# The last third of a written-out order: other neighbours for TensorE, other engines for some words, other PSUM slots

## The chip, the cores and the metric

The kernel runs on one core of one Trainium2 chip. The metric is device time in microseconds, the median of several runs. TensorE (PE) multiplies matrices out of SBUF into PSUM, VectorE (DVE) and ScalarE (ACT) do elementwise work, GpSimd (POOL) issues the DMAs that add while they move, and SyncE (SP) issues all other DMAs. Each engine takes its own instructions in order and meets the others through semaphores. PE's array is used in tiles: whole (128x128), or in parts of 128x64, 128x32, 64x128 or 64x64 rows by columns. Every matmul carries its tile; two neighbours with different tiles are a change of tile.

## The reference

A gated linear recurrence with complex decay feeds a maxout network of three branches.

```python
mag = np.sqrt(a_re * a_re + a_im * a_im)
scale = np.minimum(mag, 0.999) / (mag + 1e-06)
a_re_n, a_im_n = (a_re * scale, a_im * scale)
for t in range(S):
    ar, ai = (a_re_n[:, :, t, :, None], a_im_n[:, :, t, :, None])
    new_re = ar * S_re - ai * S_im
    new_im = ar * S_im + ai * S_re
    kv = np.einsum('bhd,bhe->bhde', k[:, :, t], v[:, :, t])
    S_re, S_im = (new_re + kv, new_im)
    y[:, :, t] = np.einsum('bhd,bhde->bhe', q[:, :, t], S_re)
...
x = np.ascontiguousarray(attn_out.transpose(0, 2, 1, 3)).reshape(B * S, H * D)
h = np.maximum(np.maximum(x @ w1, x @ w2), x @ w3)
return (h @ w_out).astype(np.float32)
```

The sizes are 4 batches, 8 heads, 768 steps, head width 48; x is 3072 by 384, the hidden width 768; all is float32.

## The kernel before

The 768 steps of a sequence are cut into six pieces of 128, and two batches go together, so that there are twelve groups (0 to 11), each with two halves x and y of 128 tokens. A group goes through these stages:

- loads: `Lr`, `Li` (a_re and a_im, one DMA of 192 KB for each half), `Lk`, `Lq`, `Lv` (four DMAs of 48 KB for each half), all on SP;
- gates on whole groups (`sqr`, `sqi`, `add`, `lnL`, `expw`, `expe`, `lne`, `relu`, `Lnop`, `abs`, `addw`, `lnw`, `expL`, `mulai`, `mulw`, `stt`, `xor`, `half`, `atan`, `turn`): logarithms of the magnitudes and the angles. `Lnop` and `addw` are adds; as a rule a DMA on POOL does them;
- sums over time as matmuls: `sums`, `F` (logarithms) and `cs` (angles), then exponentials (`En`, `Ek`, `Eq`, `f0` to `f3`) on ACT and sines (`t`, `nf`, `af`, `sa`, `sb`). `Cd` carries an angle into the next piece by a small DMA on POOL;
- `mk`, `mq`, `uk`, `uq`: k and q times decay and turned by the angle, on DVE; `tpk`, `tpq`: transposes on PE; `Kc`, `Qc`: copies of these from PSUM;
- `A`, `B`: scores on PE, which `g0` to `g3` (DVE, predicated copies) and `b0`, `b1` (ACT) put together in `atm`; `dk` and `h0` to `h3`: the state; `y`: outputs on PE; `x`: their copy into the features;
- the network: `U01` to `U12` on PE (two halves of the hidden width by three branches), `u01` to `u12` the maxima, then the output product in Strassen's form: `S1` to `S4` on DVE, products `P1` to `P7`, `Px`, `Py` on PE, sums `r1`, `r6`, `r75`, `r57`, `ox`, `oy` on DVE (r1 on ACT), and `Dx`, `Dy`, the output DMAs on SP.

Nothing of this order is left to a scheduler. `SCHEDULE` is a text of 1880 words, each a stage and its group, such as `U01:7`; `run` (called for each word in turn) issues that stage's instructions, and the class `Bound` ties every instruction of an engine to the one before it. So the words give the order on each of the five engines, and how the engines interleave follows from semaphores. Two more lists go with it. `SLOTS` has one digit for each of 304 PSUM tiles in the order in which they are asked for: which of four slots of two banks (0, 2, 4, 6) the tile takes; the first matmul of a tile waits until the last reader of the tile before it in that slot is done. `OTHER` names the words that do not run on their usual engine: copies, absolute values, maxima and `relu` then go to DVE instead of ACT, `Lnop` and `addw` to DVE instead of a DMA of POOL.

```python
ps = psum.tile([P, 2, 512], FP, tag="ps" + next(slots), name=nm)
...
(pool if other() else dve).memset(t[L64 // 2:L64], 0.0)
...
if other():
    dve.tensor_copy(out=out, in_=in_)
else:
    act.copy(out=out, in_=in_)
```

Each k or q half has one SBUF buffer (`kqs`), which the next group's load may fill after `uk` or `uq` has read it; v has four buffers, a_re and a_im two each. Nearly all instructions carry line 201, that of the helper that issues them, so the profile is read by tile names: `up` is a U product, `op` the P products, `xhx` features and hidden values, `ot` the output rows, `tp` transposes.

Around the words that the prediction follows, before:

```
... tpky:8 P5:6 ... QGy:7 g0y:7 g1y:7 ... tpkx:8 ... Lqx:9 ... Lix:10 ... Lvx:8 ... Lkx:9 ... U11:7 ... mkx:9 ... U01:7 ... turn:9 ... tpqy:8 ... u02:7 ... Fx:9 ... Lqy:9 Lky:9
... Ax:10 ... U02:9 ... U12:9 Bx:10 atan:11 Cdy:10 Cdx:10 turn:11 Ay:10 ... yx:10 QBy:10 g0y:10 g1y:10 g2y:10 xx:10 S3:9 csy:11 csx:11 ... g3y:10
```

Of the kernel before, what the change touches and what calls it, by code (L numbers as in the profile page):

```python
# [91 lines left out]
Ekx:9 Lix:10 Lvx:8 sqi:10 Lkx:9 mkx:9 Eqx:9 QBx:8 u11:7 mqx:9 Q2x:8 U01:7 Cdx:8 atan:9 u01:7 add:10 lnL:10 Eqy:9 expe:10
U02:7 turn:9 tpqy:8 Qcy:8 dkx:8 relu:10 u02:7 h1x:8 Fx:9 Dy:6 h2x:8 Dx:6 f1x:9 f0x:9 Ax:8 h3x:8 Bx:8 g0x:8 g1x:8 U12:7
g2x:8 g3x:8 lne:10 Q2y:8 f3x:9 b0x:8 f2x:9 h0x:9 Lqy:9 Q1y:8 csy:9 ty:9 u12:7 S3:7 csx:9 nfy:9 expw:10 tx:9 b1x:8 S1:7
P1:7 r1:7 QBy:8 S2:7 nfx:9 KBy:8 sbx:9 afy:9 Ay:8 g0y:8 g1y:8 afx:9 g2y:8 g3y:8 Lky:9 yx:8 xx:8 sax:9 say:9 ukx:9 abs:10
By:8 h0y:8 sby:9 mky:9 P6:7 uqx:9 P7:7 mqy:9 P5:7 r6:7 S4:7 Py:7 b0y:8 Px:7 r75:7 r57:7 QGy:8 P4:7 oy:7 tpqx:9 tpkx:9
Lnop:10 Kcx:9 b1y:8 sumsx:10 kEnx:9 Qcx:9 Q1x:9 dky:8 h1y:8 h2y:8 h3y:8 Enx:10 uky:9 addw:10 lnw:10 Lkx:10 P2:7 expL:10
P3:7 Ekx:10 ox:7 KBx:9 yy:8 xy:8 Fy:9 f0y:9 f1y:9 QGx:9 f2y:9 Lvx:9 f3y:9 dkx:9 Eqx:10 QBx:9 U01:8 mkx:10 u01:8 Q2x:9
Ax:9 xor:10 half:10 h1x:9 Lvy:9 Bx:9 uqy:9 h2x:9 h3x:9 U11:8 g0x:9 Liy:11 g1x:9 Dy:7 g2x:9 g3x:9 Lqx:10 mqx:10 Cdy:9
u11:8 Fx:10 b0x:9 b1x:9 tpky:9 tpqy:9 kEny:9 Lry:11 mulw:10 mulai:10 stt:10 Dx:7 f1x:10 f3x:10 Qcy:9 Kcy:9 Q2y:9 U02:8  # L100
u02:8 f2x:10 U12:8 Lrx:11 sqr:11 Cdx:9 S3:8 atan:10 turn:10 f0x:10 Lix:11 yx:9 sqi:11 add:11 lnL:11 xx:9 expe:11 csy:10
xor:11 ty:10 csx:10 u12:8 S1:8 KBy:9 sumsy:10 nfy:10 Eny:10 Eky:10 S2:8 Q1y:9 QBy:9 afy:10 Eqy:10 Lqy:10 dky:9 P5:8
tx:10 lne:11 P6:8 P7:8 Ay:9 h0y:9 nfx:10 h1y:9 By:9 QGy:9 h2y:9 h3y:9 g0y:9 sbx:10 g1y:9 g2y:9 relu:11 afx:10 sax:10
ukx:10 g3y:9 P1:8 S4:8 r1:8 say:10 sby:10 mqy:10 r6:8 r75:8 b0y:9 b1y:9 expw:11 Py:8 P4:8 r57:8 Px:8 uqx:10 yy:9 xy:9
Fy:10 abs:11 f2y:10 Lky:10 oy:8 tpkx:10 kEnx:10 tpqx:10 f0y:10 f1y:10 f3y:10 uqy:10 Qcx:10 Lnop:11 P2:8 Dy:8 mky:10
Kcx:10 Q1x:10 addw:11 QGx:10 Lvx:10 P3:8 ox:8 U11:9 QBx:10 u11:9 sumsx:11 Enx:11 sumsy:11 half:11 uky:10 tpqy:10 Ekx:11
Q2x:10 Eqx:11 Lkx:11 tpky:10 Qcy:10 Kcy:10 Q2y:10 mkx:11 kEny:10 KBx:10 Lqx:11 U01:9 mqx:11 u01:9 Eny:11 h0x:10 dkx:10
h1x:10 Lvy:10 Eqy:11 Eky:11 lnw:11 expL:11 Fx:11 Ax:10 h2x:10 h3x:10 f3x:11 Q1y:10 f0x:11 U02:9 g0x:10 f2x:11 g1x:10
g2x:10 Dx:8 mulw:11 g3x:10 mulai:11 stt:11 f1x:11 U12:9 Bx:10 atan:11 Cdy:10 Cdx:10 turn:11 Ay:10 b0x:10 u02:9 u12:9
b1x:10 yx:10 QBy:10 g0y:10 g1y:10 g2y:10 xx:10 S3:9 csy:11 csx:11 S1:9 Lqy:11 P1:9 Lky:11 g3y:10 ty:11 mky:11 nfy:11  # L110
afy:11 say:11 S2:9 tx:11 nfx:11 P7:9 sby:11 P5:9 P6:9 uky:11 KBy:10 By:10 h0y:10 b0y:10 dky:10 Fy:11 mqy:11 b1y:10 S4:9
r1:9 sbx:11 h1y:10 h2y:10 h3y:10 afx:11 sax:11 r6:9 Px:9 Py:9 P2:9 P3:9 QGy:10 f0y:11 r75:9 uqy:11 r57:9 f2y:11 f3y:11
Lvx:11 uqx:11 Lvy:11 P4:9 yy:10 oy:9 ox:9 tpqx:11 f1y:11 xy:10 Qcx:11 ukx:11 tpkx:11 tpky:11 Kcy:11 tpqy:11 Qcy:11
U01:10 Q2y:11 u01:10 Q1x:11 QGx:11 Kcx:11 U11:10 Dx:9 QBx:11 h0y:11 Q2x:11 kEnx:11 KBx:11 U02:10 u11:10 kEny:11 dky:11
dkx:11 u02:10 S3:10 Ax:11 Dy:9 g0x:11 Q1y:11 h0x:11 h1x:11 h1y:11 U12:10 u12:10 Ay:11 S1:10 g0y:11 g1y:11 g1x:11 Bx:11
P1:10 g2x:11 P7:10 P5:10 g3x:11 b1x:11 b0x:11 yx:11 xx:11 QBy:11 g2y:11 g3y:11 KBy:11 By:11 S2:10 S4:10 P6:10 r1:10
# [6 lines left out]
0240624024202406402024604642064262624062046420640426240260620406404624624620620260264064262464046042
0624060202264204602604204624604602204600406204240620420460246260246202460246024062624640406204602602
6402466024240642460246026042064264064240246060206426040260046024240604204060420602640424062420242002
4202
# [916 lines left out]
```

## Time and profile before

| | us |
|---|---|
| median of 3 runs | 559.31 |
| lowest and highest of them | 558.40, 559.51 |
| the profiled execution | 555.22 |
| its span, first to last instruction | 553.2 |
| PE busy | 523.6 |
| DVE busy | 482.1 |
| ACT busy | 368.2 |

The profiled execution is one more run, and the span leaves out what lies before the first and after the last instruction, 2.0 us. In the rows of the profile an instruction reads "start, duration, engine, line, operation, out<-in, shapes, count"; neighbours of one kind are merged, so x54 are 54 instructions. PE runs a float32 matmul in two passes, so that a U product of 9 matmuls shows as 18. Ends of matmuls are modelled, their starts are measured.

### The profile page before, as it was taken

How to read it: one execution, taken by the hardware profiler on the slowest of the kernel's cores; microseconds unless marked ns; L12 is line 12 of the kernel's file. 1: busy time of each engine (PE TensorE's matmuls, PEld its weight loads, DVE VectorE, ACT ScalarE, POOL GpSimd, SP SyncE). 2: the span in 40 equal slices, each digit the busy share in tenths (PEclk: the TensorE clock that was granted, in tenths of full speed). 3: DMA queues.
4: the chain of work that ended last, by engine and by line, in shares of the span. 5: the costliest groups of instructions: out<-in, count | busy, mean ns of one | idle time of the engine just before them, and what ended most of it. 6: DMA issues, size and time to landing. Idle time of an engine off the chain costs nothing.

```text
span 553.2 us, 22687 instructions
## 1 busy us (share of the span) xinstructions
PE 523.6 (95%) x10086; PEld 448.1 (81%) x10086; DVE 482.1 (87%) x752; ACT 368.2 (67%) x653; POOL 70.8 (13%) x113
## 2 busy tenths in 40 slices
PE   2669799999999999999999999999999999999996
PEld 1355697788888888888988988988988988898985
DVE  4999999999999997999988888999999998887432
ACT  7999987777867787868776768786637835520100
POOL 7224140030020020000210200120020020000000
PEclk9979999999999999999999999999999999999999
DMA  8989774262616332324353245542361153000000
GB/s 203 295 246 176 174 131 79 50 128 63 109 38 124 67 68 51 61 44 88 72 121 58 35 85 108 101 91 54 62 125 20 32 105 72 2 31 2 31 1 28
DMA packets 141953, 47.51 MB, mean 86 GB/s; under 512 B 130464, under 2 KB 135584, under 8 KB 141856
## 3 DMA queue, kind: packets, MB, share of 16 engines
q1 hardware_dynamic: 136272, 37.77, 31.5%
q0 software_dynamic: 5584, 8.30, 8.9%
q8 instruction: 79, 1.29, 1.0%
q14 instruction: 18, 0.15, 0.1%
HBM read 33.03 MB, written 4.72 MB: 68 GB/s over the span
## 4 chain that ended last, share of the span: by engine, by line
PE 84%; DVE 7%; ACT 4%; SPq 2%; issue 1%; DMA 1%; DVEq 0%; ACTq 0%
PE up L201 33%; PE op L201 24%; PE y L201 7%; PE A L201 5%; PE tp L201 4%; PE dk L201 3%; PE sums L201 2%; PE cs L201 2%; DVE w L201 2%; SPq L201 2%; PE F L201 2%; PE B L201 1%; DMA wo<-in_moe_w_dram 1%; DVE atm L201 1%; ACT f L201 1%
## 5 line engine op out<-in xcount | busy, mean ns | idle before, releaser
L201 PE MATMUL up<-xhx,w 128*128 128x256 f32 x792 | 177.0, 382 | 0.1
L201 PEld LDWEIGHTS up<-xhx,w 128*128 128x128 f32 x792 | 148.6, 190 | 21.5 <-PE B L201 0.3
L201 ACT ACT_TABLE_LOAD x49 | 62.9, 1283 | 1.6 <-PEq L1027 0.8
L201 ACT COPY atm<-B 32x128 f32<-32x128 f32 x96 | 24.6, 256 | 37.8 <-DVE atm L201 19.7
L201 PE MATMUL op<-wo,xhx 128*128 128x192 f32 (+1 forms) x220 | 48.4, 363 | 0.0
L201 DVE TENSOR_TENSOR Q<-Q,f 112x1024 f32<-112x1024 f32 (+1 forms) x48 | 45.4, 952 | 1.7 <-ACT Q L201 1.2
L201 POOL DMA_DIRECT2D ar<-nf x40 | 34.6, 1305 | 60.3 <-DVE ar L201 48.9
L201 ACT ACTIVATE f<-F 48x232 f32<-48x232 f32 x96 | 34.5, 359 | 10.1 <-PE F L201 6.1
L201 PEld LDWEIGHTS op<-wo,xhx 128*128 128x128 f32 x220 | 36.5, 190 | 4.6 <-issue 0.6
L201 PE MATMUL y<-atm,vb 128*32 128x64 f32 x1152 | 39.0, 221 | 0.2 <-ACT K L201 0.2
L201 PE MATMUL y<-QG,g 112*32 112x64 f32 x1408 | 38.0, 219 | 0.2 <-issue 0.2
L201 PEld LDWEIGHTS y<-atm,vb 128*32 128x32 f32 x1152 | 32.4, 109 | 5.3 <-issue 2.9
L201 PEld LDWEIGHTS y<-QG,g 112*32 112x32 f32 x1408 | 34.8, 109 | 0.3 <-issue 0.3
L201 DVE TENSOR_TENSOR ot<-ot,op 128x384 f32<-128x384 f32 (+1 forms) x56 | 25.6, 464 | 10.7 <-PE op L201 6.4
L201 PE MATMUL op<-wo,strassen 128*128 128x192 f32 x176 | 33.0, 331 | 0.0
L201 POOL DMA_DIRECT2D Ln<-e x9 | 8.3, 923 | 192.2 <-ACT e L201 53.8
L201 PE MATMUL A<-Q,K 112*32 112x80 f32 x1536 | 31.6, 234 | 1.4 <-DVE Q L201 1.4
L201 DVE COPY_PREDICATED atm<-masko,A 128x256 f32<-128x256 uint8 x72 | 31.2, 435 | 1.7
L201 PE MATMUL op<-w,strassen 128*128 128x192 f32 x176 | 32.2, 329 | 0.0
L201 PEld LDWEIGHTS A<-Q,K 112*32 112x32 f32 x1536 | 27.3, 110 | 4.2 <-issue 3.1
L201 PEld LDWEIGHTS op<-wo,strassen 128*128 128x128 f32 x176 | 28.8, 190 | 0.8
L201 ACT COPY Q<-tp 112x1024 f32<-112x1024 f32 x22 | 22.3, 1014 | 10.7 <-PE tp L201 10.5
(148 smaller groups left out, 1080.5 us busy)
## 6 DMA issues: line engine op xcount, KB each, us to landing
ar<-in_a_re_dram SPq DMA_DIRECT2D x24, 192.0 KB, 3.1
...
q<-in_q_dram SPq DMA_DIRECT2D x96, 48.0 KB, 2.6
k<-in_k_dram SPq DMA_DIRECT2D x96, 48.0 KB, 2.6
vb<-in_v_dram SPq DMA_DIRECT2D x96, 48.0 KB, 3.0
...
```

Of the source, the lines that this page charges most:

```text
L201: ins = f(*a, **kw)
```

## The change

From word 1309 on (`Lrx:10` before, `Lky:9` after) the same 571 words stand in another order. In the built programs PE changes its tile 189 times before and 185 times after. `SLOTS` has the same 304 digits in number, but differs from the 66th on (word 449, `dkx:2`). In `OTHER` 22 words are gone and 26 are new, 27 of the 48 with a place ahead of word 1309. Words, stages and sizes stay. Of the order, the places that matter here (the whole text is 50 lines):

```diff
-S2:6 P6:6 nfx:8 Q1y:7 QBy:7 Lky:8 mky:8 By:7 afx:8 uky:8 sbx:8 Ay:7 abs:9 Lnop:9 tpky:8 Lrx:10 QGy:7 g0y:7 g1y:7 g2y:7
+S2:6 P6:6 nfx:8 Q1y:7 QBy:7 Lky:8 mky:8 By:7 afx:8 uky:8 sbx:8 Ay:7 abs:9 Lnop:9 tpky:8 Lky:9 Lrx:10 QGy:7 g0y:7 g1y:7
...
+f0y:8 expL:9 half:9 mulai:9 Cdy:8 f2y:8 f3y:8 Eny:9 Lvx:9 Liy:10 mulw:9 QGx:8 stt:9 U11:7 KBx:8 Eky:9 uqy:8 Lry:10
+sqr:10 Lqx:9 Ekx:9 Lix:10 Lvx:8 sqi:10 Lkx:9 mkx:9 Eqx:9 Lqy:9 QBx:8 u11:7 mqx:9 Q2x:8 U01:7 Cdx:8 atan:9 u01:7 add:10
+lnL:10 Eqy:9 expe:10 U02:7 turn:9 tpqy:8 Qcy:8 dkx:8 relu:10 mky:9 h0y:8 u02:7 h1x:8 Fx:9 Dy:6 h2x:8 Liy:11 Lry:11
...
+f3x:11 Eky:11 f0x:11 Eny:11 Eqy:11 Ay:10 Ax:10 Bx:10 g0y:10 g1y:10 stt:11 g0x:10 g1x:10 g2x:10 g3x:10 Cdy:10 Cdx:10
+atan:11 turn:11 h0x:11 U12:9 h0y:10 g2y:10 g3y:10 b1x:10 b0x:10 csx:11 csy:11 yx:10 tx:11 ty:11 QBy:10 u12:9 KBy:10
...
-u01:11 U11:11 U02:11 u11:11 u12:11 P1:11 S3:11 Dy:10 u02:11 S1:11 S2:11 Px:11 P2:11 P5:11 S4:11 P6:11 r1:11 r6:11 Py:11
-P3:11 P7:11 r75:11 ox:11 P4:11 Dx:11 r57:11 oy:11 Dy:11
+r57:10 oy:10 u02:11 P3:10 u12:11 S1:11 S3:11 P1:11 P5:11 ox:10 S2:11 Dx:10 Dy:10 Px:11 P6:11 r1:11 P2:11 Py:11 r6:11
+S4:11 P7:11 P3:11 r75:11 r57:11 ox:11 P4:11 Dx:11 oy:11 Dy:11
```

The words that change engine, by list:

```diff
-u01:2 afx:3 afy:4 abs:4 addw:6 u01:7 afx:7 abs:7 u11:7 xy:8 relu:8 u11:8 relu:9 afx:9 Kcy:9 abs:9 Kcx:10 afy:10 u01:11 Kcy:11 xy:11 Kcx:11
+afy:2 u11:3 afy:3 afx:4 relu:5 xx:5 u11:5 Qcx:5 Kcx:6 relu:6 xx:6 u11:6 xx:7 abs:8 afx:8 afy:8 Lnop:8 Qcy:9 u11:9 xx:10 Lnop:10 relu:10 u01:10 afy:11 Qcy:11 Lnop:11
```

A word with a minus ran on DVE before and runs on ACT after (addw on POOL's DMA); one with a plus the other way round. `relu` on DVE leaves the constant out that ACT's form adds, and `lne` of that group puts it in. The PSUM slots that the prediction speaks of: `Fx:9` takes the slot of `sumsy:9` before and of `U02:7` after; `csy:11` takes that of `Bx:10` before and of `Ay:10` after.

More of the change, by code (lines that the diff above doesn't have):

```diff
@@ L87 @@
 dky:7 S1:6 h1y:7 h2y:7 csx:8 csy:8 tx:8 ty:8 nfy:8 h3y:7 afy:8 yx:7 xx:7 P7:6 relu:9 expw:9 KBy:7 say:8 sby:8 Lqy:8 P1:6
-S2:6 P6:6 nfx:8 Q1y:7 QBy:7 Lky:8 mky:8 By:7 afx:8 uky:8 sbx:8 Ay:7 abs:9 Lnop:9 tpky:8 Lrx:10 QGy:7 g0y:7 g1y:7 g2y:7
-sax:8 Kcy:8 P5:6 S4:6 g3y:7 ukx:8 r1:6 uqx:8 mqy:8 r6:6 h0x:8 b0y:7 r75:6 r57:6 b1y:7 Px:6 P2:6 P3:6 Py:6 P4:6 kEny:8
-tpkx:8 ox:6 oy:6 addw:9 lnw:9 tpqx:8 yy:7 Qcx:8 sumsx:9 Kcx:8 kEnx:8 xy:7 Fy:8 Q1x:8 sumsy:9 Enx:9 xor:9 f1y:8 f0y:8
-expL:9 half:9 mulai:9 Cdy:8 f2y:8 f3y:8 Eny:9 Liy:10 mulw:9 QGx:8 stt:9 U11:7 KBx:8 Eky:9 uqy:8 Lry:10 sqr:10 Lqx:9
@@ L92 @@
[L92 to L116, printed above, removed]
@@ L117 @@
-r6:10 b0y:11 Px:10 P2:10 Py:10 P4:10 QGy:11 b1y:11 r75:10 r57:10 oy:10 yy:11 xy:11 P3:10 ox:10 Dx:10 U12:11 U01:11
-u01:11 U11:11 U02:11 u11:11 u12:11 P1:11 S3:11 Dy:10 u02:11 S1:11 S2:11 Px:11 P2:11 P5:11 S4:11 P6:11 r1:11 r6:11 Py:11
-P3:11 P7:11 r75:11 ox:11 P4:11 Dx:11 r57:11 oy:11 Dy:11
+S2:6 P6:6 nfx:8 Q1y:7 QBy:7 Lky:8 mky:8 By:7 afx:8 uky:8 sbx:8 Ay:7 abs:9 Lnop:9 tpky:8 Lky:9 Lrx:10 QGy:7 g0y:7 g1y:7
+g2y:7 sax:8 Kcy:8 P5:6 S4:6 g3y:7 ukx:8 r1:6 uqx:8 mqy:8 r6:6 h0x:8 b0y:7 r75:6 r57:6 b1y:7 Px:6 P2:6 P3:6 Py:6 P4:6
@@ new lines @@
+kEny:8 tpkx:8 ox:6 oy:6 addw:9 lnw:9 tpqx:8 yy:7 Qcx:8 sumsx:9 Kcx:8 kEnx:8 xy:7 Fy:8 Q1x:8 sumsy:9 Enx:9 xor:9 f1y:8
+f0y:8 expL:9 half:9 mulai:9 Cdy:8 f2y:8 f3y:8 Eny:9 Lvx:9 Liy:10 mulw:9 QGx:8 stt:9 U11:7 KBx:8 Eky:9 uqy:8 Lry:10
+sqr:10 Lqx:9 Ekx:9 Lix:10 Lvx:8 sqi:10 Lkx:9 mkx:9 Eqx:9 Lqy:9 QBx:8 u11:7 mqx:9 Q2x:8 U01:7 Cdx:8 atan:9 u01:7 add:10
+lnL:10 Eqy:9 expe:10 U02:7 turn:9 tpqy:8 Qcy:8 dkx:8 relu:10 mky:9 h0y:8 u02:7 h1x:8 Fx:9 Dy:6 h2x:8 Liy:11 Lry:11
+Lix:11 Lvy:9 Lrx:11 Dx:6 lne:10 csy:9 ty:9 f1x:9 f2x:9 f3x:9 Q1y:8 nfy:9 Ax:8 g0x:8 g1x:8 Lnop:10 g2x:8 Q2y:8 h3x:8
@@ new lines @@
+U12:7 u12:7 g3x:8 S1:7 sby:9 f0x:9 S2:7 Bx:8 Ay:8 xor:10 S3:7 g0y:8 g1y:8 P1:7 csx:9 r1:7 b1x:8 expw:10 tx:9 nfx:9 afy:9
+afx:9 sax:9 sbx:9 b0x:8 abs:10 P6:7 P7:7 P5:7 Py:7 Px:7 KBy:8 h0x:9 QBy:8 S4:7 r6:7 ukx:9 r75:7 g2y:8 P4:7 r57:7 uqx:9
+g3y:8 yx:8 QGy:8 oy:7 By:8 dky:8 xx:8 b1y:8 b0y:8 tpkx:9 tpqx:9 addw:10 Qcx:9 P2:7 P3:7 sumsx:10 Kcx:9 h1y:8 kEnx:9
+Q1x:9 h2y:8 dkx:9 ox:7 Q2x:9 h1x:9 h3y:8 yy:8 Ax:9 Eqx:10 say:9 xy:8 Enx:10 sqr:11 lnw:10 Ekx:10 expL:10 U01:8 u01:8
+U11:8 mqy:9 uky:9 h2x:9 QGx:9 KBx:9 half:10 uqy:9 mulai:10 h3x:9 mulw:10 QBx:9 g0x:9 g1x:9 g2x:9 g3x:9 Cdx:9 Cdy:9 u11:8
@@ new lines @@
+Lvx:10 Dx:7 Lky:10 Lqy:10 Lkx:10 Dy:7 Lqx:10 Bx:9 tpqy:9 tpky:9 b1x:9 b0x:9 stt:10 Qcy:9 Kcy:9 sumsy:10 Fy:9 Fx:10 f2y:9
+f0y:9 f0x:10 f1y:9 f3y:9 U02:8 f3x:10 sqi:11 f1x:10 kEny:9 Eny:10 Eky:10 atan:10 add:11 lnL:11 f2x:10 Eqy:10 u02:8 Q1y:9
+KBy:9 Q2y:9 U12:8 yx:9 turn:10 csx:10 csy:10 tx:10 xx:9 ty:10 u12:8 S1:8 mqy:10 QBy:9 S2:8 nfx:10 nfy:10 Ay:9 g0y:9
+g1y:9 mqx:10 g2y:9 QGy:9 S3:8 By:9 dky:9 h0y:9 h1y:9 g3y:9 mkx:10 h2y:9 afy:10 sby:10 sbx:10 say:10 uqy:10 afx:10 P5:8
+P6:8 P7:8 P1:8 Py:8 P4:8 Px:8 expe:11 lne:11 r1:8 relu:11 b0y:9 b1y:9 sax:10 S4:8 r6:8 r75:8 h0x:10 mky:10 r57:8 oy:8
@@ new lines @@
+uky:10 Lnop:11 uqx:10 h3y:9 ukx:10 Fy:10 yy:9 f1y:10 xy:9 f0y:10 f2y:10 f3y:10 expw:11 P2:8 P3:8 ox:8 tpkx:10 kEnx:10
+tpqy:10 tpqx:10 tpky:10 Kcx:10 Qcx:10 Kcy:10 Qcy:10 abs:11 addw:11 dkx:10 sumsx:11 Eqx:11 lnw:11 Enx:11 Ekx:11 QGx:10
+U11:9 Q1y:10 QBx:10 Q2x:10 h1x:10 Q1x:10 xor:11 kEny:10 h2x:10 u11:9 Q2y:10 Dx:8 Lky:11 Lkx:11 Dy:8 Lqx:11 U01:9 U02:9
+u01:9 expL:11 mulai:11 Lqy:11 Lvx:11 Lvy:10 half:11 KBx:10 h3x:10 mulw:11 u02:9 mqx:11 Fx:11 sumsy:11 f1x:11 f2x:11
+f3x:11 Eky:11 f0x:11 Eny:11 Eqy:11 Ay:10 Ax:10 Bx:10 g0y:10 g1y:10 stt:11 g0x:10 g1x:10 g2x:10 g3x:10 Cdy:10 Cdx:10
@@ new lines @@
+atan:11 turn:11 h0x:11 U12:9 h0y:10 g2y:10 g3y:10 b1x:10 b0x:10 csx:11 csy:11 yx:10 tx:11 ty:11 QBy:10 u12:9 KBy:10
+nfy:11 nfx:11 S3:9 xx:10 S1:9 mkx:11 By:10 Fy:11 dky:10 h1y:10 b1y:10 sby:11 sbx:11 b0y:10 afx:11 sax:11 P1:9 Px:9 Py:9
+P2:9 mky:11 h2y:10 afy:11 h3y:10 P7:9 P5:9 uqx:11 QGy:10 S2:9 S4:9 P6:9 P3:9 P4:9 say:11 f0y:11 uky:11 f2y:11 r1:9
+f3y:11 ukx:11 f1y:11 r6:9 r75:9 r57:9 mqy:11 oy:9 uqy:11 yy:10 xy:10 ox:9 tpky:11 tpkx:11 tpqy:11 tpqx:11 Kcy:11 kEnx:11
+Qcy:11 kEny:11 Qcx:11 QBx:11 Q1y:11 Q1x:11 U11:10 U01:10 u01:10 u11:10 Kcx:11 U02:10 QGx:11 Q2x:11 u02:10 KBx:11 S3:10
@@ new lines @@
+Q2y:11 U12:10 u12:10 Bx:11 Ax:11 g0x:11 g1x:11 Ay:11 g0y:11 g1y:11 S1:10 g2x:11 g3x:11 S2:10 h0y:11 P1:10 P7:10 P5:10
+Lvy:11 Dx:9 Dy:9 b1x:11 b0x:11 dky:11 dkx:11 g2y:11 P6:10 h1y:11 h1x:11 QBy:11 KBy:11 S4:10 g3y:11 yx:11 r1:10 r6:10
+QGy:11 r75:10 By:11 b1y:11 xx:11 Px:10 P2:10 Py:10 b0y:11 yy:11 xy:11 P4:10 U11:11 U01:11 u11:11 u01:11 U02:11 U12:11
+r57:10 oy:10 u02:11 P3:10 u12:11 S1:11 S3:11 P1:11 P5:11 ox:10 S2:11 Dx:10 Dy:10 Px:11 P6:11 r1:11 P2:11 Py:11 r6:11
+S4:11 P7:11 P3:11 r75:11 r57:11 ox:11 P4:11 Dx:11 oy:11 Dy:11
@@ L120 @@
 """
 SLOTS = """
[L123 to L126, printed above, removed]
+0240624024202406402024604642064262624062046420640426240260620406424604604602602062064260464060260264
+2046202424406246062064264024064062260644246042024604204262046062064020642064206240406462624024620260
@@ L127 @@
+4260244602026424624606246002462442060420642062640240624640264026264024640260426026042060620462206002
+0226
 """
 OTHER = set("""
-Zf:0 Zg:0 afx:0 relu:1 Qcy:0 addw:2 Lnop:2 Wg8:0 u21y:0 addw:3 relu:4 afx:3 abs:4 Lnop:4 u01:2 xx:3 afy:4 afx:5 addw:6
-u01:4 afx:6 afy:6 abs:7 relu:8 Kcy:6 afy:7 afx:7 relu:9 abs:9 u11:7 u01:7 afx:9 Kcx:9 xy:8 u11:8 Kcy:9 afy:10 abs:11
-Kcx:10 Qcy:10 Kcy:11 Kcx:11 xy:11 u01:11 u11:11
+Zf:0 Zg:0 afx:0 relu:1 Qcy:0 addw:2 Lnop:2 Wg8:0 u21y:0 afy:2 addw:3 relu:4 afy:3 Lnop:4 xx:3 relu:5 afx:4 u11:3 afx:5
@@ L133 @@
+relu:6 Qcx:5 u01:4 afx:6 afy:6 xx:5 Kcx:6 u11:5 Lnop:8 Kcy:6 afy:7 xx:6 abs:8 u11:6 afy:8 xx:7 afx:8 relu:10 Lnop:10
+Kcx:9 Qcy:9 abs:11 Lnop:11 u11:9 Qcy:10 xx:10 afy:11 Qcy:11 u01:10 u11:11
 """.split())
```

## The prediction

> **What bounds the kernel now.** I read the page from the top: busy times, the slices, the chain. TensorE (PE) is the bound, and VectorE (DVE) is a hair behind it.
>
> ```profile
> PE 523.6 (95%) x10086; PEld 448.1 (81%) x10086; DVE 482.1 (87%) x752; ACT 368.2 (67%) x653; POOL 70.8 (13%) x113
> PE   2669799999999999999999999999999999999996
> DVE  4999999999999997999988888999999998887432
> PE 84%; DVE 7%; ACT 4%; SPq 2%; issue 1%; DMA 1%; DVEq 0%; ACTq 0%
> ```
>
> From the sixth slice on PE is never below nine tenths until the last slice, and the chain that ended last runs through PE for 84% of the span. How much of that is waiting, and how much room the others have, the waits of PE from 60 us on and a table of busy time by stretch say:
>
> ```profile
> PE A L201 <- DVE Q L201: 1.4, 1, 1.4
> PE op L201 <- DVE ot L201: 1.2, 1, 1.2
> ...
> PE dk L201 <- DVE nf L201: 1.0, 1, 1.0
> ...
> 200.00:280.00 80.00, 79.93 (x1599) 70.57 (x1601) 72.46 (x113) 61.87 (x105) 5.89 (x7) 1.00 0.38 73
> 280.00:352.00 72.00, 71.85 (x1439) 62.58 (x1434) 62.44 (x97) 54.51 (x96) 5.88 (x7) 1.00 0.43 83
> 352.00:480.00 128.00, 127.93 (x2635) 112.06 (x2625) 120.23 (x186) 78.68 (x146) 14.13 (x17) 1.00 0.34 65
> ```
>
> In a stretch's row the figures after its length are the busy times of PE, PE's weight loads, DVE, ScalarE (ACT) and GpSimd (POOL). PE's named waits are four, of 1.0 to 1.4 us, 4.6 in 493 us. Word 1309 falls at 352 us. From there to 480 us PE idles 0.1 us, DVE 7.8 and ACT 49. So there is almost nothing to take back from waits: a new order can win only what PE itself does less, and lose whatever makes PE wait. The granted clock is 1.00 in all three rows.
>
> **The changes of tile.** The words after 1309 are the same words; nothing is computed more or less. In the built program's order of matmuls the tile of the array changes 189 times before and 185 times after, all four fewer behind word 1309. What one costs:
>
> ```profile
> 364.47 11.92 PE L201 MATMUL up<-xhx,w 128*128 128x256 f32 x54
> 376.32 0.66 PE L201 MATMUL tp<-ident,uq 64*112 64x64 f32 x16
> ...
> 378.33 1.31 PE L201 MATMUL A<-Q,K 112*32 112x80 f32 x64
> 379.46 0.48 PE L201 MATMUL B<-QB,KB 112*32 112x32 f32 x32
> 380.01 4.12 PE L201 MATMUL up<-xhx,w 128*128 128x256 f32 x18
> ...
> 457.43 1.31 PE L201 MATMUL A<-Q,K 112*32 112x80 f32 x64
> 458.67 8.04 PE L201 MATMUL up<-xhx,w 128*128 128x256 f32 x36
> 466.64 0.46 PE L201 MATMUL B<-QB,KB 112*32 112x32 f32 x32
> 466.91 1.33 PE L201 MATMUL A<-Q,K 112*32 112x80 f32 x64
> ```
>
> I take starts, since ends are modelled. 54 up matmuls take 376.32 - 364.47 = 11.85 us, 36 take 466.64 - 458.67 = 7.97. The difference, 3.88, is 18 matmuls alone, so one visit to the full array costs 7.97 - 2 x 3.88 = 0.21 for going in and out. An A followed by B, which has the same tile, takes 379.46 - 378.33 = 1.13; followed by up it takes 1.24: leaving a small tile costs 0.11. Behind word 1309 full-array stretches fall by three (21 entries to 18), while changes between small tiles rise by two (18 to 20). Three round trips at 0.21 + 0.11 are 0.96; two small changes cost 0.11 to 0.2 each, 0.3. That gives **-0.6 us** (bounds -0.4, four of the cheapest, and -0.8, four of the dearest at 0.21).
>
> **The last words.** Before, P7:11 is PE's last product but one and P4:11 waits until ox:11 is done, since both use one PSUM tile; ox:11 stands on DVE behind r75:11, which needs P7:11.
>
> ```profile
> 546.81 1.41 DVE L201 TENSOR_TENSOR ot<-ot,op 128x384 f32<-128x384 f32 x3 [2.50 <-PE op L201]
> 548.01 1.57 PE L201 MATMUL op<-w,xhx 128*128 128x192 f32 x8 [1.23 <-DVE ot L201]
> ```
>
> The three DVE adds are r75, ox and r57, and PE goes on after the second. After, P7:11 comes ahead of P3:11, so r75:11 and r57:11 run beside P3:11's 1.3 us, and only ox:11 is left between P3:11 and P4:11: one add of 128x384 goes from the path. The two took 548.01 - 546.81 = 1.20, 0.6 each with PE's release in it: **-0.55 us**, bounds -0.5 and -0.6. Behind P4:11 nothing changes.
>
> **SP's queue: Lkx:9.** This is the step I trust least. Lky:9 and Lvx:9, four DMAs each, and Lrx:10, Liy:10 and Lry:10, one each, now stand in one run ahead of Lqx:9. Lky:9 waits for the uky:8 multiply that reads its buffer, so the run starts when that ends, and Lkx:9, which mkx:9 on DVE waits for, is the last four of its 24 issues.
>
> ```profile
> 350.67 0.96 DVE L201 TENSOR_TENSOR uk<-CS,k 128x768 f32<-128x768 f32 x1
> ...
> 370.72 0.55 DVE L201 TENSOR_TENSOR k<-Ek,k 128x384 f32<-128x384 f32 x1
> 371.19 0.69 DVE L201 TENSOR_TENSOR QB<-Q,f 112x512 f32<-112x512 f32 x1
> ...
> 357.50 2.58 SPq L201 DMA_DIRECT2D q<-in_q_dram  x4
> 360.13 0.60 SPq L201 DMA_DIRECT2D ai<-in_a_im_dram  x1
> 360.77 3.84 SPq L201 DMA_DIRECT2D vb<-in_v_dram  x4
> 364.65 2.59 SPq L201 DMA_DIRECT2D k<-in_k_dram  x4
> ...
> 241.86 0.36 SPq L201 DMA_DIRECT2D out_dram<-ot  x1
> ...
> 259.12 0.55 SPq L201 DMA_DIRECT2D ai<-in_a_im_dram  x1
> ...
> k<-in_k_dram SPq DMA_DIRECT2D x96, 48.0 KB, 2.6
> ...
> 377.79 0.23 PE L201 MATMUL F<-cuts,Ln 64*48 64x29 f32 x2
> ```
>
> uky:8 ends at 351.63. Before, the 13 issues from Lqx:9 to Lkx:9 took 364.65 + 2.59 - 357.50 = 9.74 us. The 11 new ones take 2.58 to 3.84 for each four and 0.6 for each single one, 7.0 at the least, so Lkx:9's last would be issued at 351.63 + 9.74 + 7.0 - 0.65 = 367.7 and land 2.6 later, at 370.3: no wait. The nearest whole row is the run of 24 issues from 241.86 to 259.67 (20 loads of 48 KB, two of 192, two outputs), 17.8 us. It is taken, because it has the count: 351.63 + 17.8 - 0.65 + 2.6 = 371.4. mkx:9's turn comes at 370.72, so DVE waits 0.7. The other end: a four that stalls costs 1.3 more (3.84 against 2.58); three more of them put the landing at 375.3, a wait of 4.6.
>
> Queued behind mkx:9 on DVE are QBx:8, mqx:9, Q2x:8, add:10, turn:9, relu:10, mky:9, h0y:8 and u02:7, and Fx:9 on PE waits for u02:7, which empties the PSUM slot that Fx:9 takes in the new list. The next instruction on DVE starts 0.08 before the one ahead ends (0.55 long, 371.19 - 370.72 = 0.47 to the next). With that, u02:7 ends at 370.72 + 0.47 + 0.61 + 0.47 + 1.14 + 2 x 0.87 + 3 x 0.47 + 0.95 = 377.5, and Fx:9 starts at 377.79: 0.2 to spare. So PE waits 0.7 - 0.2: **+0.5 us** (0 to 4.4).
>
> The Trainium skill, DMA: Bandwidth & Descriptors, section Bandwidth, speaks against this step: it has transfers under 64 KB dominated by their descriptors, not by their bytes. The trace agrees in that four loads of 48 KB take SP 0.65 each and one of 192 KB takes 0.60; what it makes of the whole run is rival 3.
>
> **DVE between Ay:10 and csy:11.** The new list puts csy:11 into the PSUM slot of A(10, y), which is free after g3y:10; before it took that of Bx:10. Between Ay:10's last matmul and csy:11 PE has Ax:10 (1.13), Bx:10 (0.27 from 466.64 to 466.91, and 0.11 for leaving), U12:9 (384.06 - 380.01 = 4.05) and csx:11:
>
> ```profile
> 384.06 1.52 PE L201 MATMUL cs<-w,upto 128*64 128x192 f32 x16
> 385.52 1.57 PE L201 MATMUL op<-wo,xhx 128*128 128x192 f32 x8
> ...
> 379.78 0.72 DVE L201 COPY_PREDICATED atm<-maskd,A 128x512 f32<-128x512 uint8 x1
> 380.54 1.39 DVE L201 COPY_PREDICATED atm<-masko,A 128x256 f32<-128x256 uint8 x3
> 381.83 1.22 DVE L201 TENSOR_TENSOR Q<-Q,f 112x1024 f32<-112x1024 f32 x1
> ```
>
> Two cs take 385.52 - 384.06 = 1.46, the first some 0.7: a cover of 6.25 us. DVE must do in that time g0y, g1y, stt:11, g0x, g1x, g2x, g3x, turn:11, h0x:11, h0y:10, g2y, g3y. A first predicated copy steps 0.76 (380.54 - 379.78), three that follow each other 1.29 (0.48, 0.48 and 0.33 where another word follows). So 0.76 + 0.33 + 0.87 + 0.76 + 1.29 + 0.87 + 2 x 0.47 + 0.48 + 0.44 = 6.74, and about 0.2 for PE's last matmul to end (they are shown 0.22 long, each counted to the next start) and release DVE: 6.95. csy:11 is late by **+0.7 us** (0 if the copies need not wait for one another, 0.9 if DVE is behind already). No other matmul stands ahead of csy:11 that PE could do meanwhile.
>
> **What is moved between engines.** 48 words change engine, 27 of them ahead of word 1309, and PSUM slots differ from the 66th of 304 on, word 449. Ahead of 1309 17 words come to DVE and 10 leave it.
>
> ```profile
> L201 DVE COPY K<-tp 112x1024 f32<-112x1024 f32 x3 | 3.7, 1220 | 0.1
> L201 DVE TENSOR_SCALAR xhx<-up 128x768 f32<-128x768 f32 x3 | 2.9, 953 | 0.8 <-PE up L201 0.8
> L201 ACT ACT_TABLE_LOAD x12 | 15.4, 1283 | 0.2
> ```
>
> With copies of K and Q at 1.22, maxima at 0.95 and the rest shorter, DVE gains some 5.6 us net by word 1309 and loses some 3 behind it. I cost this at nothing: most of the 5.6 falls between 200 and 352 us, where DVE idles 7.5 + 9.6 us by the rows above. If that cover fails it is 5.6 us of PE waiting. Six more table loads, 7.7 us of ACT, lie in ACT's 49. Small waits come and go: 0 with +-0.5 (PE's named waits of 3.4 beside the tail's, over 493 us, are 1.4 in 200).
>
> **Sum:** -0.6 - 0.55 + 0.5 + 0.7 + 0 = +0.05 on the profiled execution's 555.22 us (span 553.2, 2.0 around it), 555.3. It stands 4.1 below the runs' median of 559.31; the difference is carried over: **559.4 us**.
>
> **Rivals.** (1) Both new waits stay away and the gains stand: 559.31 - 0.6 - 0.55, 558.2 us. For it: both waits are under a microsecond by my own sums, and DVE has 7.8 us free from 352 to 480. Against: each needs something to go better than its nearest row. (2) SP's run of 24 issues stalls more than the row taken, and mkx:9 becomes the place where PE loses: from a landing at 372.5 on the whole is slower. With three more stalled fours 559.3 - 1.15 + 4.4 + 0.7 = 563.3 us; midway 561.3. For it: no run of SP over 13 issues in these rows is free of a stall, and DVE has no gap behind mkx:9. Against: k loads land in 2.6 us at the median. (3) The run is paced by its pieces of 192 bytes, so that a load of 192 KB weighs as four of 48: the row of 17.8 us holds 20 + 2 x 4 such units, the new run 20 + 4 x 4, and takes 17.8 x 36 / 28 = 22.9 us; mkx:9 is 5.8 late, PE 5.6, the time 564.5 us. Against: the two sizes take SP the same. The skill's rule above is of this kind. (4) DVE becomes the bound between 200 and 352 us: if half of the 5.6 is not covered, 562.2. For it: DVE's slices there are eights and nines; against: 17 us of idle. (5) The change does not do what it says: its lists also differ ahead of word 1309, but the four tile changes are gone from the order; with nothing else 559.3, the forecast's own class.
>
> **Chances.** Forecast, with (5), 0.46; rival 1 0.17; rival 2 0.22; rival 3 0.05; rival 4 0.10. A measurement of this kernel tells 0.2%, 1.1 us, from no change. So faster 0.17, since rival 1 stands just at that edge; same 0.46; slower 0.37. Range 557.9 to 562.4: down to all gains at their better bounds, up past the midpoints of rivals 2 and 4; what is left out is rival 3 and the far ends of the other two, some 0.2. The forecast's own range is 558.2 to 560.4.
>
> **What would show it.** Tile changes: a visit of up still 0.21, PE's busy work shorter by half a microsecond. Tail: one DVE add, not two, between P3:11's end and P4:11. Lkx:9: an idle DVE just before the k multiply near 370.7, released by a DMA, and F at 378.4 in place of 377.8. csy:11: a wait of cs for DVE's atm near 468. Wrong would be PE waits over a microsecond anywhere between 100 and 352 us, or DVE waiting for a load elsewhere.

## The result, and the profile after

The changed kernel takes 562.46 us (median of 6 runs, 561.00 to 564.38), the kernel before 558.81 us in 6 runs. The ratio is 1.0066 with a 95% interval of 1.0044 to 1.0088: slower by 3.65 us, where 559.4 and no change were predicted. The profiled execution of the changed kernel took 562.00 us, span 560.3.

The two traces differ by more than the medians, 560.3 against 553.2. The first 1309 words tell little of that. The table of stretches, for the kernel before and then for the changed one, begins here at the first matmul of word 1308 (tpky:8), which is the same word in both, and goes to the end:

```profile
352.50:480.50 128.00, 127.93 (x2609) 112.17 (x2605) 120.23 (x186) 79.16 (x147) 14.13 (x17) 1.00 0.34 65
480.50:553.20 72.70, 67.84 (x942) 60.62 (x940) 39.64 (x60) 9.43 (x21) 0.00 (x0) 0.99 0.05 18
```

```profile
354.40:482.40 128.00, 123.09 (x2577) 107.34 (x2573) 114.60 (x178) 87.50 (x153) 11.61 (x14) 1.00 0.33 63
482.40:560.30 77.90, 73.66 (x974) 66.00 (x972) 40.93 (x65) 12.43 (x26) 0.00 (x0) 1.00 0.05 17
```

From there to the end it is 200.7 us before and 205.9 after, 5.2 more. The 1.9 us ahead of it need not be the change's: a second execution of the kernel before (below) comes to that word at 354.69, too. In the first 128 us of the stretch PE idles 0.07 us before and 4.9 after, at a granted clock of 1.00 in both. So PE waits. For what, the list of PE's waits from 350 us on says (who waited, for whom, us in total, times, longest; the first six rows). Before, it held one row, that of the tail, 1.2 us:

```profile
PE tp L201 <- ACT Eq L201: 1.5, 1, 1.5
PE B L201 <- issue: 1.1, 1, 1.1
PE y L201 <- issue: 1.1, 1, 1.1
PE op L201 <- DVE ot L201: 0.6, 1, 0.6
PE cs L201 <- DVE atm L201: 0.5, 1, 0.5
PE F L201 <- DVE xhx L201: 0.3, 1, 0.3
```

Three things are new. The first is the k load. Four views of the changed kernel follow, SP's queue, DVE, ACT and PE in order of time:

```profile
353.92 3.29 SPq L201 DMA_DIRECT2D k<-in_k_dram  x4
...
369.63 3.23 SPq L201 DMA_DIRECT2D k<-in_k_dram  x4
```

```profile
371.75 0.95 DVE L201 TENSOR_TENSOR uq<-CS,q 128x768 f32<-128x768 f32 x1
374.89 0.56 DVE L201 TENSOR_TENSOR k<-Ek,k 128x384 f32<-128x384 f32 x1 [2.18 <-DMA k<-in_k_dram]
...
377.57 0.95 DVE L201 CUSTOM_DVE_ANT_0 L<-L,e 128x768 f32<-128x768 f32 x1
```

```profile
378.55 0.84 ACT L201 ACTIVATE L<-L 128x768 f32<-128x768 f32 x1 [2.00 <-DVE L L201]
379.30 0.47 ACT L201 ACTIVATE Eq<-sums 128x384 f32<-128x384 f32 x1
```

```profile
366.37 11.92 PE L201 MATMUL up<-xhx,w 128*128 128x256 f32 x54
379.83 0.66 PE L201 MATMUL tp<-ident,uq 64*112 64x64 f32 x16 [1.53 <-ACT Eq L201]
380.42 1.14 PE L201 MATMUL dk<-vb,uk 64*64 64x48 f32 x64
381.85 0.56 PE L201 MATMUL F<-cuts,Ln 64*48 64x29 f32 x32 [0.28 <-DVE xhx L201]
```

They show one delay that is handed on through four queues. The run of 24 issues takes SP from 353.92 to 372.86, and its last load, Lkx:9, lands at some 374.8. mkx:9 on DVE has waited 2.18 us for it. add:10 stands behind mkx:9 on DVE, lnL:10 on ACT waits for add:10, Eqy:9 stands behind lnL:10, and tpqy:8 on PE needs the PSUM slot that Eqy:9 empties: 1.53 us of PE. Fx:9 then waits for u02:7 as well.

The second is csy:11, the third two gaps in the middle of a word:

```profile
474.07 0.87 PE L201 MATMUL cs<-w,upto 128*64 128x192 f32 x8
475.48 0.87 PE L201 MATMUL cs<-w,upto 128*64 128x192 f32 x8 [0.54 <-DVE atm L201]
...
477.89 0.36 PE L201 MATMUL B<-QB,KB 112*32 112x32 f32 x21
479.37 0.32 PE L201 MATMUL B<-QB,KB 112*32 112x32 f32 x11 [1.12 <-issue]
```

csy:11 starts 1.41 after csx:11, where two cs stand 0.70 apart without a wait: 0.71 late, for g3y:10. By:10 stops after 21 of its 32 matmuls; "issue" means that no semaphore explains the wait. yy:8 stops the same way at 409 us. At the end, from the start of P3:11's last matmul to P4:11's first weight load 0.97 us pass in the trace, against 1.56 from P7:11's in the kernel before.

### The profile page after: what moved, and what is told of

It is laid out like the page before. It is cut to its first block, busy times and chain, and to the rows that moved or that the text cites. A ratio compares the mean times of both kernels' runs of the same rounds, so it can differ in the third digit from the quotient of the medians.

```text
span 560.3 us, 22670 instructions
## 1 busy us (share of the span) xinstructions
PE 524.6 (94%) x10086; PEld 448.8 (80%) x10086; DVE 482.7 (86%) x756; ACT 375.3 (67%) x657; POOL 69.2 (12%) x111
## 4 chain that ended last, share of the span: by engine, by line
PE 74%; DVE 13%; SPq 4%; ACT 3%; DMA 3%; issue 3%; DVEq 0%; ACTq 0%
PE up L201 28%; PE op L201 22%; PE y L201 6%; PE A L201 4%; SPq L201 4%; PE tp L201 3%; PE dk L201 3%; DVE w L201 3%; DVE atm L201 2%; PE cs L201 2%; PE sums L201 2%; DMA xhx<-in_moe_w_dram 2%; PE F L201 1%; PE B L201 1%; DVE uk L201 1%
## 5 line engine op out<-in xcount | busy, mean ns | idle before, releaser
L201 DVE TENSOR_TENSOR xhx<-xhx,up 128x768 f32<-128x768 f32 x22 | 20.9, 952 | 13.8 <-PE up L201 13.7
L201 ACT COPY K<-tp 112x1024 f32<-112x1024 f32 x21 | 21.3, 1012 | 13.2 <-PE tp L201 12.9
L201 PEld LDWEIGHTS op<-w,strassen 128*128 128x128 f32 x176 | 28.9, 190 | 1.1 <-issue 0.3
```

The source lines that it names most:

```text
L201: ins = f(*a, **kw)
```

## The experiments

Theories at the start: the loss lies behind word 1309 in waits that belong to the new order (k load 2.1 us, csy:11 0.7, stops inside words 2.6 to 2.9), less 1.1 gained; rival: part of it is chance, or comes from the moves of engines and slots ahead of word 1309.

### Both kernels once more

> The kernel before once more, for a second profiled execution. Theory (the new order makes PE wait, and the waits belong to the order): the trace again shows PE without a wait of over 0.5 us between 120 and 540 us; where this execution is longer than the 553.2 us of the first, the difference lies in the first 100 us, where loads and weights set the pace. Rival (waits of PE come and go from one execution to the next): waits of 1 us and more appear behind 352 us here too, at other words than in the changed kernel.

> The changed kernel once more. Theory: the same waits as in its first trace at the same words: DVE about 2 us for Lkx:9 ahead of mkx:9, PE 1.5 ahead of tpqy:8, 1.3 inside yy:8 and 1.3 inside By:10 that no semaphore explains, 0.7 ahead of csy:11; ratio to the kernel before 1.005 to 1.008. Rival (the two waits inside a word are chance): they are gone or inside other words, while the three others stay, and the ratio is nearer 1.003.

The kernel before: 557.40 us, span 555.4. It comes to tpky:8 at 354.69 instead of 352.51, and from there to the end takes 200.71 us against 200.69. PE's list of waits from 110 to 545 us has one row:

```profile
PE y L201 <- issue: 0.2, 1, 0.2
```

The changed kernel: 560.62 against 557.14 us, ratio 1.0069 (1.0047 to 1.0090), 205.45 us from tpky:8 on. Its list from 350 to 545 us:

```profile
PE tp L201 <- ACT Eq L201: 1.8, 1, 1.8
PE y L201 <- issue: 1.1, 1, 1.1
PE B L201 <- issue: 0.6, 1, 0.6
PE cs L201 <- DVE atm L201: 0.5, 1, 0.5
PE F L201 <- DVE xhx L201: 0.3, 1, 0.3
```

The same words wait. Only the stop in By:10 is shorter. So the waits belong to the order, and the lengths of the stops vary.

### What the stops are

The page's table of DMA queues has a row that is the same in both kernels: queue, kind, packets, MB, share.

```profile
q8 instruction: 79, 1.29, 1.0%
```

79 packets of 16384 bytes, on a queue of instructions. Counting PE's weight loads, matmuls and semaphore instructions in the trace in order of start, there are some 20,300, 79 pieces of 256, 64 bytes each. The stops of the changed kernel stand at places 15297 and 18113 of that count: both 193 more than a multiple of 256. So they are at the ends of pieces, and what differs between the orders is how long PE takes for a piece: matmuls of A, B, y, dk and F are short, 256 instructions of them take 2 us; a U product has 36 in 4 us.

```
kernel          piece ends in   PE took for the piece   stop (us)
after           By:10           1.72                    1.31
after           By:8            1.80                    0.30
after           yy:8            2.27                    1.31
after_again     By:10           1.73                    0.76
after_again     By:8            1.80                    0.24
after_again     yy:8            2.27                    1.31
before, shortest behind word 1309
                dky:9           3.60                    0.02
```

To test it, the kernel before, whose order, engines and slots stay, gets 20 small matmuls more at 34 us:

```diff
-                            mm(out=ps[o:o + D, ch, (2 * i + j) * NF:(2 * i + j + 1) * NF],
...
+                            n = 4 * (2 * i + j) + 2 * u + ch
+                            for _ in range(1 + (20 + 15 - n) // 16 if x == 1 else 1):
+                                mm(out=ps[o:o + D, ch, (2 * i + j) * NF:(2 * i + j + 1) * NF],
...
```

> The kernel before with 20 of Fy:0's small matmuls issued once more (near 34 us, where PE waits anyway): order, engines and slots stay, only PE's instructions after them stand 80 places later. The trace loads PE's code in pieces of 16384 bytes, 79 of them. Theory (PE stops for 1.3 us where it comes to the end of a piece less than some 2.2 us after the end of the one before): with the ends 80 instructions further on, nine pieces behind 60 us last 1.7 to 2.3 us (at the words run near 113, 185, 265, 303, 376, 387, 402, 455 and 466 us) where before there was one: stops of 1.3 us at most of them, 8 to 12 us more, 567 to 571 us. Rival (the two stops inside words of the changed kernel have nothing to do with where code lies): 558.8 us as before, 0.5 more at most for the matmuls themselves.

Measured: 579.75 against 557.14 us, ratio 1.0391 (1.0350 to 1.0433), where 567 to 571 us were expected. PE's waits from 110 us on, the largest four:

```profile
PE y L201 <- issue: 3.2, 3, 1.4
PE B L201 <- issue: 3.0, 3, 1.2
PE dk L201 <- issue: 2.5, 3, 1.0
PE A L201 <- issue: 2.1, 2, 1.1
```

No row of the list names a semaphore. Behind 110 us there are 18 stops of over 0.4 us, 18.3 us in all, every one at place 193 of 256. The mechanism holds; its size was off by a factor of two, since I had counted pieces under 2.3 us only, and those of 2.4 to 2.8 stop PE as well.

The control adds 64 matmuls, one whole piece:

> The kernel before with 64 of Fy:0's matmuls more in place of 20: 256 instructions of PE, one whole piece of 16384 bytes. Theory (where the ends of pieces fall in the order decides): every end of a piece falls where it falls in the kernel before, so the stops of the kernel with 20 more are gone although more is added: 557 to 559 us, up to 1.5 us over the kernel before if the 64 matmuls are not hidden. Rival (the repeated matmuls themselves, or a PE that starts out of step, cost the 22 us): as slow as with 20, or slower, 1.03 and more.

Measured: 561.51 against 556.91 us, ratio 1.0083 (1.0054 to 1.0111), more than the 557 to 559 us expected. But all of it lies ahead: from tpky:8 on it is 200.85 us, as in the kernel before. What is slow is the addition itself (the rows are of PE, and of the stretch from 30 to 40 us):

```profile
34.80 8.56 PE L201 MATMUL F<-cuts,Ln 64*48 64x29 f32 x160
```

```profile
30.00:40.00 10.00, 8.87 (x197) 8.73 (x198) 9.74 (x15) 7.64 (x11) 1.86 (x3) 0.50 0.88 243
```

Fy:0 alone takes 8.5 us, 0.053 for each of 160 matmuls; with 20 more it was 2.16, 0.030 for each of 72. The granted clock does not tell the two apart, it was 0.50 during Fy:0 in both. Here each matmul of the word stands five times in a row, there two or three times; whether that is the reason was not tried. Behind 110 us PE's list of waits has one row of 0.2 us again, and the row of q8 now counts 80 packets: the 256 instructions more are one packet more. Three times the addition, and no stop of over 0.5 us behind it: where the pieces end decides.

The same was tried on the changed kernel with Lvx:9 moved (next section), with 7 matmuls more, 28 instructions.

> The changed kernel with Lvx:9 behind Lqy:9, and 7 of Fy:0's matmuls more near 34 us: 28 instructions of PE, so that each end of a piece lies 28 instructions earlier in the order. Theory: the stops move and their words can be named: none in By:8 and yy:8 any more (pieces that end there last 3 us and more), new ones in Ax:9 (a piece of 1.97 us) and dky:9 (1.91 us), at most a small one in By:10; the sum of the stops about the same, the time within 1 us of the kernel without the 7, ratio 1.002 to 1.006. Rival (the stops belong to the words yy:8 and By:10, whatever the reason): they stay where they were.

Measured: 566.13 against 557.42 us, ratio 1.0159 (1.0122 to 1.0195), well above the 1.002 to 1.006 expected. The list from 110 to 545 us:

```profile
PE dk L201 <- issue: 1.6, 1, 1.6
PE F L201 <- issue: 1.6, 1, 1.6
PE A L201 <- issue: 1.5, 1, 1.5
PE y L201 <- issue: 1.0, 1, 1.0
PE cs L201 <- DVE atm L201: 0.5, 1, 0.5
PE op L201 <- issue: 0.5, 1, 0.5
```

Ax:9 and dky:9 stop as named, By:8 and By:10 do not any more. But yy:8 still stops, though its piece lasts 3.6 us, and two stops came that I had not named. So the time for a piece is not the whole rule. In yy:8's case the load of the piece began 2.5 us after PE had entered the piece before; the middle half of the loads of all traces begins 0.4 to 1.1 us after that, some up to 4 us ahead, a few up to 6 us after. Put together over the 13 traces of this study, behind 100 us: at 82 ends of pieces PE paused over 0.23 us, and in 75 of these it went on 1.20 to 1.60 us after the end of the load that brings the next piece; the other seven are one place, a pause of 0.25 us long after its load. At the other ends, some 820, PE was never nearer to the end of that load than 1.22 us. That is the rule that these traces show: PE enters a piece no sooner than 1.2 us after its load has ended, and as the load begins at about the time when the piece before is entered, that piece must last long enough.

The Trainium skill, Runtime: NRT & Kernel Launch, section Instruction fetch mechanics, has the refill in blocks of 16 KiB, 256 instructions, and the next block fetched while the present one runs; these traces agree, with 79 loads of 16384 bytes. It calls the cost of a block's end mostly hidden; in the trace with 20 matmuls more it was 18.3 us of 576.3, and there the measurement decides.

### The k load

```diff
-f0y:8 expL:9 half:9 mulai:9 Cdy:8 f2y:8 f3y:8 Eny:9 Lvx:9 Liy:10 mulw:9
+f0y:8 expL:9 half:9 mulai:9 Cdy:8 f2y:8 f3y:8 Eny:9 Liy:10 mulw:9
...
-sqr:10 Lqx:9 Ekx:9 Lix:10 Lvx:8 sqi:10 Lkx:9 mkx:9 Eqx:9 Lqy:9 QBx:8
+sqr:10 Lqx:9 Ekx:9 Lix:10 Lvx:8 sqi:10 Lkx:9 mkx:9 Eqx:9 Lqy:9 Lvx:9 QBx:8
```

> The changed kernel with Lvx:9 (four DMAs) behind Lqy:9 instead of ahead of Liy:10, so that Lkx:9 is issued some 3.7 us earlier. Theory: Lkx:9 lands near 371.2 in place of 374.9, mkx:9 does not wait, the 1.5 us ahead of tpqy:8 and the 0.5 ahead of Fx:9 are gone: 2.0 us less than the changed kernel, ratio to the kernel before near 1.003. Rival (the k load only took the place of another wait, or PE would have waited there anyway): no gain, ratio as that of the changed kernel, 1.005 to 1.008.

Measured: 559.67 against 557.14 us, ratio 1.0039 (1.0014 to 1.0064), beside 1.0069 for the changed kernel on the same chip: 1.7 us less by the ratios, 0.95 by the medians. From tpky:8 to the end it is 203.54 us, 1.9 less than 205.45. DVE and PE in order of time:

```profile
371.90 0.95 DVE L201 TENSOR_TENSOR uq<-CS,q 128x768 f32<-128x768 f32 x1
372.76 0.55 DVE L201 TENSOR_TENSOR k<-Ek,k 128x384 f32<-128x384 f32 x1
```

```profile
366.52 11.92 PE L201 MATMUL up<-xhx,w 128*128 128x256 f32 x54
378.37 0.66 PE L201 MATMUL tp<-ident,uq 64*112 64x64 f32 x16
378.96 1.14 PE L201 MATMUL dk<-vb,uk 64*64 64x48 f32 x64
380.01 0.56 PE L201 MATMUL F<-cuts,Ln 64*48 64x29 f32 x32
```

mkx:9 follows uq without a gap, tpqy:8 starts 11.85 after the three U products and Fx:9 right behind dkx:8. The theory's 2.0 is met in the trace; in the times the gain is seen less surely, since the intervals of the two ratios overlap.

### The last third alone

Order, engines and slots of the kernel before for 1309 words, those of the changed kernel behind. (PSUM tiles have the same owners at the cut; the four slots are only named in another turn, 6, 0, 2, 4 for 0, 2, 4, 6.)

> The first 1309 words with the engines and PSUM slots of the kernel before, the words behind with order, engines and slots of the changed kernel. Theory (all of the loss lies behind word 1309): ratio to the kernel before as that of the changed kernel, 1.005 to 1.008, with the same waits at tpqy:8, yy:8, csy:11 and By:10. Rival (the engine and slot changes ahead of word 1309 cost part of it): 1.000 to 1.003.

Measured: 562.37 against 556.91 us, ratio 1.0081 (1.0054 to 1.0108). 204.70 us from tpky:8 on, and waits at the same words (tp 1.0, B 0.9, y 0.8, cs 0.6, F 0.3). So the changes of engines and slots ahead of word 1309 are not needed for the loss, and cost nothing that can be seen.

### The tail alone

```diff
-P3:11 P7:11 r75:11 ox:11 P4:11 Dx:11 r57:11 oy:11 Dy:11
+P7:11 P3:11 r75:11 r57:11 ox:11 P4:11 Dx:11 oy:11 Dy:11
```

> The kernel before with the changed kernel's last nine words alone (P7:11 ahead of P3:11, r57:11 ahead of ox:11). Theory: PE waits some 0.8 us between its last two products instead of 1.4: ratio 0.999, in the trace the gap ahead of P4:11 1.0 in place of 1.56. Rival (Dx:11 or r57:11 takes the gain back behind P4:11): the gap shrinks and the end stays, 1.000.

> The kernel before with the changed kernel's last nine words once more, for a second interval. Theory: 0.6 us less, ratio 0.999. Rival: 1.000.

Measured: ratio 0.9986 (0.9968 to 1.0004), then 1.0010 (0.9979 to 1.0041). From tpky:8 to the end 200.67 us: nothing gained. PE's last rows say why:

```profile
544.21 0.81 PE L201 MATMUL op<-wo,xhx 128*128 128x384 f32 x2
545.22 1.57 PE L201 MATMUL op<-w,strassen 128*128 128x192 f32 x8 [0.20 <-DVE ot L201]
546.62 1.46 PE L201 MATMUL op<-wo,strassen 128*128 128x192 f32 x8
548.73 1.57 PE L201 MATMUL op<-w,xhx 128*128 128x192 f32 x8 [0.65 <-DVE ot L201]
```

The gap ahead of P4:11 shrinks to 0.97 as expected, but P7:11 now starts 1.01 after Py:11, which takes 0.65: it waits for r6:11, which reads the tile that P7:11 writes, and P3:11 no longer covers that. In the changed kernel P2:11 stands in between. So the last words with P2:11 and S4:11 behind P6:11:

```diff
-Px:11 P2:11 P5:11 S4:11 P6:11 r1:11 r6:11 Py:11 P3:11 P7:11 r75:11 ox:11 P4:11 Dx:11 r57:11 oy:11 Dy:11
+Px:11 P5:11 P6:11 r1:11 P2:11 r6:11 Py:11 S4:11 P7:11 P3:11 r75:11 r57:11 ox:11 P4:11 Dx:11 oy:11 Dy:11
```

> The kernel before with its last words in the changed kernel's manner, and P2:11 and S4:11 behind P6:11 as there (Px P5 P6 r1 P2 r6 Py S4 P7 P3 r75 r57 ox P4 Dx oy Dy). In the kernel with the last nine words alone P7:11 waited 0.68 us for r6:11, which reads the same PSUM tile; here P2:11 gives r1:11 and r6:11 the 1.3 us that they need. Theory: the wait ahead of P7:11 is gone, the one ahead of P4:11 stays at 1.0, and from tpky:8 to the end it is 200.2 us, against 200.8 in both traces of the kernel before; ratio 0.999. Rival (P5:11 or P6:11 now waits for S1:11 or S2:11 instead): 200.8 again, ratio 1.000.

Measured: 556.75 against 557.67 us, ratio 0.9980 (0.9954 to 1.0006). The wait ahead of P7:11 is gone, the gap ahead of P4:11 is 0.97. The trace has 201.49 us from tpky:8 on, not 200.2, but 1.26 of it is a stop at the end of a piece inside an F near 479 us, where that piece's load began late, 3.0 us after the piece before was entered; no other trace of the kernel before has it. Its ratio is the lowest of all versions tried, but 1 lies within the interval: a gain is not shown.

### Three repairs together

```diff
-csx:11 csy:11 yx:10 tx:11 ty:11 QBy:10 u12:9 KBy:10 nfy:11 nfx:11 S3:9
+csx:11 yx:10 csy:11 tx:11 ty:11 QBy:10 KBy:10 u12:9 nfx:11 nfy:11 S3:9
...
-sumsx:10 Kcx:9 h1y:8 kEnx:9 Q1x:9 h2y:8 dkx:9 ox:7
+Kcx:9 h1y:8 kEnx:9 Q1x:9 h2y:8 dkx:9 sumsx:10 ox:7
```

and Lvx:9 behind Lqy:9 as above. (The lines are parts of lines of the order; the digits of `SLOTS` move with their words.)

> The changed kernel with three repairs: Lvx:9 behind Lqy:9 as in the earlier run; csy:11 behind yx:10 on PE (with KBy:10 ahead of u12:9 and nfy:11 behind nfx:11 on DVE), so that csy:11 need not wait for g3y:10 and a slow word stands in the run of small ones; sumsx:10 behind dkx:9, so that the piece of code that ends inside yy:8 holds the whole of a slow word. Theory: 2.0 us less from the first, some 1.0 from the second (then DVE is the limit there), 0.5 to 1.0 from the third; ratio to the kernel before 0.999 to 1.002. Rival (the lost time moves on to the next wait): 1.003 as with the first repair alone, or above.

Measured: 558.66 against 556.91 us, ratio 1.0019 (1.0000 to 1.0038); 202.49 us from tpky:8 on. PE's waits from 110 to 545 us:

```profile
PE y L201 <- issue: 0.8, 1, 0.8
PE F L201 <- DVE nf L201: 0.3, 1, 0.3
```

csy:11's wait is gone, and of By:10's stop 0.34 us are left. The third repair failed: yy:8's piece now lasts 2.43 us and PE still stops for 1.03 at its end. Of the 4.8 us from tpky:8 on (205.45 less 200.7) the repairs of the first two kinds bring back 3.0.

## Why the prediction was wrong, step by step

Two steps failed. The larger one is a term that the sum lacked: the prediction looked for waits on semaphores alone and put nothing down for the arrival of PE's code, and PE stopped 2.9 us at three ends of pieces in the first trace, 2.3 in the second. The other is the term for Lkx:9, sized at 0.5 and measured at 2.0, since the delay was followed along DVE only and not into ACT's queue. The other terms came out within 0.3 of their size.

**The bound** was right: PE, with nothing to win back from waits.

**The tiles.** Predicted -0.6. Take for each kind of word the shortest time that PE spends on it in the 13 traces, one for words ahead of a full-array word and one for the rest. What PE takes beyond that grows by 6.2 us up to the last U product, and shrinks by 0.6 behind it; the whole grew by 5.2, so the words themselves take 0.4 less. With the words told apart by the tile of the next one, it is 0.3 less. So the sign was right and the size too large, by a reckoning: no run changed the tiles alone.

**The tail.** Predicted -0.55, measured -0.59 (0.97 less 1.56). Right in the changed kernel. What the prediction did not say is that P7:11 can stand ahead of P3:11 only because P2:11 moved as well; the tail alone showed it.

**SP's queue.** The place was right and the size was not: predicted +0.5, measured 2.0, within the bounds of 0 to 4.4: tpqy:8 starts 13.46 after U11:7 where three U products take 11.85, 1.6 late, and Fx:9 1.43 after dkx:8 where 1.05 passes with Lvx:9 moved, 0.4 late. Two terms of it. The run of 24 issues took 18.9 us, not 17.8 (rival 3 had 22.9), and DVE came to mkx:9 0.3 earlier than reckoned, 18.8 after uky:8 and not 19.1, so that DVE waited 2.18, not 0.7. And the prediction followed the delay on DVE alone, to u02:7 and Fx:9, with 0.2 to spare. It went by a shorter way: add:10 on DVE, lnL:10 and behind it Eqy:9 on ACT, whose PSUM slot tpqy:8 takes. ACT's queue is where the step failed.

**csy:11.** Predicted +0.7, measured 0.71. The prediction put the place near 468 us by mistake; it is 475.

**Moves between engines.** Predicted 0, and the cover that it named held: beside the rows of the prediction, DVE does 5.4 us more between 200 and 352 us, and PE is as busy as before in both stretches.

```profile
200.00:280.00 80.00, 79.83 (x1534) 70.07 (x1528) 73.75 (x113) 60.44 (x102) 6.76 (x9) 1.00 0.40 76
280.00:352.00 72.00, 71.93 (x1478) 62.86 (x1475) 66.60 (x103) 52.23 (x92) 5.15 (x7) 1.00 0.38 71
```

A PE wait of over a microsecond between 100 and 352 us was named as a sign of being wrong, and there is one: at 101.5 us PE stops inside a y, 1.1 us by its list of waits and 0.2 before. It, too, is at the end of a piece, and the time at which tpky:8 is reached does not show it.

**What was not in it.** The prediction took an instruction's slot from rows of before and looked for waits on semaphores. That PE's code must arrive was no term of it, since in the trace of before nothing behind 110 us waits for it. Three visits to the full array fewer mean that small words stand closer together. As I read the order, the very step that was to win 0.6 made pieces of 1.72, 1.80 and 2.27 us where the shortest was 3.60, and cost 2.9 us in the first trace (1.31 + 0.30 + 1.31), 2.3 in the second.

**The sum**: -0.4 - 0.6 + 2.0 + 0.7 + 2.9, and 0.6 left over, which are waits under 0.4 us each, make the 5.2 of the trace. The medians say 3.65 (2.5 to 4.9); the ratios of the repeat and of the last third alone, 1.0069 and 1.0081, are 3.8 and 4.5 us. The three traces with this last third give 5.2, 4.7 and 4.0; how often a load comes in time differs from one execution to the next, and how the average comes to 3.65 is left open. Of the rivals, that of a later k load had the time (561.3 to 563.3), by luck in part: its place was a third of the losses, 2.0 of 6.2 us, and the stops, which it does not name, made up the rest of the time.
